# The second layer of a fused attention and MLP kernel, done for two batches at once with two levels of seven products

## The chip, the cores and the metric

The kernel runs on one core of one Trainium2 chip. The metric is the device time of one execution in microseconds (us); the time of a kernel is the median of several runs.

## The reference

Attention with normalised queries and keys is followed by an MLP with two matrix products. There are 8 batches, 12 heads, 448 positions and a head dimension of 64, so the MLP sees 8 x 448 rows of 768 numbers; its inner width is 2048. All is float32 (the weights arrive as float64).

```python
q_n, k_n = (rmsnorm(q, g_q), rmsnorm(k, g_k))
scores = scale * np.matmul(q_n, k_n.transpose(0, 1, 3, 2))
attn = np.exp(scores - np.max(scores, axis=-1, keepdims=True))
attn = attn / (np.sum(attn, axis=-1, keepdims=True) + 1e-09)
x = np.matmul(attn, v)          # then (B,H,S,D) -> (B*S, H*D)
h = x @ w_in                    # 768 -> 2048
g = h - np.tanh(h)
out = g @ w_out                 # 2048 -> 768
```

## The kernel before, in words

**Two streams on one TensorE.** The work is written out by hand in one order, in which each engine keeps its instructions. The attention is cut into 48 steps `s`, one for each batch and pair of heads (six a batch). The MLP of a batch is a Python generator (`hidden`, then `project`; `project_first` for batch 0), which yields after each matmul the time that it should take. The function `slot(s)` (from step 12 on) issues one attention step and calls `run(gap / 2)` eight times in between, which draws MLP matmuls from the generator until their time is used up. `gap_ns` says how much MLP goes into a step: from step 12 on, a sixth of a batch's MLP. The MLP of a batch runs while the attention of the next one is made; the last batch's MLP has no attention beside it.

**A slot.** It opens with the attention block on TensorE: scores of the last keys of step s+1, the values of step s, the division (`divide`, on VectorE, DVE), and the other scores of s+1, whose exponentials ScalarE (ACT) makes. After that comes one piece of DVE work between each two draws of MLP: `add` (L527, L528: sums of the exponentials over the key blocks; two instructions of 128x896), then `norm_blocks` (L458 to L463: mean squares of queries and keys, the power on GpSimd (POOL)), then `add_last` and `fold` (L535, L592, L594, and eight small copies on ACT, L598), `scale_blocks` (L470), two `turn_blocks` (L480, L484) and `spread_sums` (L606 to L611).

**The MLP.** Both layers use a scheme with seven products of half-sized blocks instead of eight (Strassen's, in Winograd's form): rows 0 to 223 and 224 to 447 of the 448 positions are the halves of one operand, halves of the inner dimension and of the output the others. `products` runs them in the `ORDER` 1, 5, 6, 2, 3, 7, 4. In the first layer (`hidden`) a block `j` (of four) has seven products of six matmuls of 224 columns; in the second (`project`) a block `j` (of three) has seven products of eight. Three PSUM banks serve the products in turn: products 1, 5, 6 and 4 take the next bank and start anew, while 2, 3 and 7 go on adding in the banks of 1, 5 and 6 after these have been read. Reading is done by `use` right after a product, on ACT for product 1 and on DVE for most others. For product 2 of the first layer it is `shrink` with `v`, the bank itself (L711 and L712: the tanh on ACT, then a subtraction on DVE, both from PSUM). A part of this work is put in `late["todo"]` and is issued after the next product's matmuls.

**The sums ahead.** The seven products need sums of blocks of the moving operand. For the first layer `divide` makes them when it has both halves (L634 to L637, on POOL). For the second layer `factors` makes them per block `j` (L722, L723 on DVE, L724 and L756 on POOL).

**The weights.** Sums of weights for both layers are made during batch 0 and kept in DRAM. From batch 1 on, tiles of weights come through a ring of six places in SBUF, loaded by SP's queue (`ring_load`, L379); a load is issued when its place has been left, which is four tiles ahead of its use. SP issues all DMAs in the order in which they are written, and waits in that order.

**Results.** `store` (L764) turns a 128x448 tile in 32x32 blocks on DVE and sends it by four DMAs.

Of the kernel before, what the change touches and what calls it, by code (L numbers as in the profile page):

```python
# [20 lines left out]
NCH = 4  # L21
# [116 lines left out]
def bounded_path(tc, ctx, q, k, v, moe_w_in, moe_w_out, out, g_col, ident, ones, half_ones, neg_half, early):  # L138
# [31 lines left out]
    HC, HF = CD // 2, CF // 2  # L170
    SETS = CF // 4
    ORDER = (1, 5, 6, 2, 3, 7, 4)
    SLOTS, SLOT = 6, 8 * P
# [16 lines left out]
    xp = pool("xp", bufs=9)  # L190
    gp = pool("gp", bufs=1)
    wp_stack = ctx.enter_context(ExitStack())
    wp = wp_stack.enter_context(tc.tile_pool(name="wp", bufs=1))
# [9 lines left out]
    def mm_bank():  # L203
        return bank_of("mm")

    loaded = {}

    def load(s, names):
        b, hp = steps[s]
        for name in names:  # L210
            src = {"q": q, "k": k, "v": v}[name]
            if s == 0 and name != "v":
                t = early[name]
            else:
                shape = [CP, 2, NCH, D] if name == "q" else [P, NCH, 2, D] if name == "k" else [P, 2, NCH, D]
                t = nat.tile(shape, F32, name=f"{name}_nat", bufs=3 if name == "v" else 2)
                fetch(nc, name, t, src[b, 2 * hp : 2 * hp + 2], by_blocks(s))
            loaded[name, s] = t
# [7 lines left out]
    }  # L226
    BLOCKS = {1: 0, 2: 1, 4: 2, 7: 3, 5: 4, 6: 5, 3: 6}
    w_out_dram = scratch.tile([P, 7, HC, HF, P], F32, name="w_out")
    w_in_words, w_out_words = weight_words(moe_w_in), weight_words(moe_w_out)
# [135 lines left out]
    def ring_slot():  # L365
# [3 lines left out]

    ring_steps = [  # L370
        (b, layer, j, p)
        for b in range(1, B)
        for layer, count in ((0, SETS), (1, HC))
        for j in range(count)
        for p in ORDER
    ]
    ring_tiles = {}

    def ring_load(to):  # L379

        for n in range(len(ring_tiles), min(to, len(ring_steps))):
            b, layer, j, p = ring_steps[n]
            t = ring_tiles[ring_steps[n]] = ring_slot()
            if layer == 0:
                assert kept[1] > j
                nc.sync.dma_start(out=t[:, : 2 * HALF], in_=w_in_dram[j, p])
            else:
                nc.sync.dma_start(out=t, in_=w_out_dram[:, BLOCKS[p], j].rearrange("p f d -> p (f d)"))

# [49 lines left out]
    def load_blocks(s):  # L439
        b, hp = steps[s]  # L440
        t = loaded["qk", s] = late["blocks"].tile([P, 2, NJ, BL], F32, name="qk_nat", bufs=2)
        for i, src in enumerate((q, k)):
            for h in range(2):
                rows = src[b, 2 * hp + h].rearrange("(j t) (m d) -> m t j d", t=BL, d=BL)
                for m in range(2):
                    r = (2 * h + m) * BL
                    nc.sync.dma_start(out=t[r : r + BL, i], in_=rows[m])
# [20 lines left out]
    def scale_blocks(s):  # L468
        n, rr = normed[s], normed.pop(("rr", s))
        nc.vector.tensor_tensor(  # L470
            out=n.rearrange("p i j d -> p (i j) d"), in0=loaded.pop(("qk", s)).rearrange("p i j d -> p (i j) d"),
            in1=rr[:, :, None].to_broadcast([P, 2 * NJ, BL]), op=ALU.mult,
        )
# [114 lines left out]
    def fold(s):  # L588

        t = sums.pop(s)[0].rearrange("p h s -> p (h s)")  # L590
        turned_sum = late["blocks"].tile([P, 2 * S], F32, name="sum_T")
        nc.vector.transpose(out=turned_sum, in_=t)  # L592
# [20 lines left out]
    def divide(s, av):  # L613
        b, hp = steps[s]
        rs = whole.pop(s)
        x = xT[b, hp] = xp.tile([P, S], F32, name="xT")
        for n in range(2):
# [6 lines left out]
        for c in range(NCH):  # L624
            del probs[s, c]
        if hp < HC:
            return
        c = hp - HC
        if c == 0:
            tt[b] = tp.tile([P, 3, HC, HS], F32, name="tt", bufs=1)  # L630
        eng = nc.vector if b == 0 and c == HC - 1 else nc.gpsimd
        x11, x12, x21, x22 = (xT[b, r][:, n : n + HS] for r in (c, hp) for n in (0, HS))
        t1, t2, t4 = (tt[b][:, i, c] for i in range(3))
        eng.tensor_tensor(out=t1, in0=x12, in1=x11, op=ALU.subtract)  # L634
        eng.tensor_tensor(out=t2, in0=x22, in1=t1, op=ALU.subtract)  # L635
        eng.tensor_tensor(out=x12, in0=x22, in1=x12, op=ALU.subtract)
        eng.tensor_tensor(out=t4, in0=x21, in1=t2, op=ALU.subtract)  # L637

# [15 lines left out]
    def products(b, layer, count, width, depth, moving, done_with):  # L654
# [8 lines left out]
        def product(j, p, bank, first):  # L663
# [20 lines left out]
            for fn in now:  # L684
                fn()

        for j in range(count):
# [8 lines left out]
    def hidden(b):  # L696

        g = late["g"] = gp.tile([P, CF, S], F32, name="gT")
        t2 = late["tg"].tile([P, 3, HF, HS], F32, name="tg") if b else None
        late["t"] = t2  # L700
        x = [xT.pop((b, c)) for c in range(CD)]
        t = tt.pop(b)
        low, high = slice(0, HS), slice(HS, S)
        moving = {
            1: lambda c: x[c][:, low], 2: lambda c: x[c + HC][:, low], 3: lambda c: x[c + HC][:, high],
            4: lambda c: t[:, 2, c], 5: lambda c: t[:, 0, c], 6: lambda c: t[:, 1, c], 7: lambda c: x[c][:, high],
        }

        def shrink(rows, cols, h, eng):
# [4 lines left out]
        def done_with(j):  # L714
# [11 lines left out]
            def use(p, bank):  # L726
                v = view(bank)
                if p == 1:
                    nc.scalar.copy(out=s1, in_=v)
# [14 lines left out]
                elif p == 4:  # L744
                    nc.vector.tensor_tensor(out=s1, in0=v, in1=s1, op=ALU.add)

                    if b and j == SETS - 1:
                        factors()

                    def rest():  # L750
                        shrink(down, low, s1, nc.gpsimd)
                        if b and j < SETS - 1:
                            factors()
                        if b:
                            g21, f2, f4 = g[:, down, low], t2[:, 1, up], t2[:, 2, up]
                            nc.gpsimd.tensor_tensor(out=f4, in0=g21, in1=f2, op=ALU.subtract)  # L756
# [7 lines left out]
    def store(b, n, y):  # L764
# [6 lines left out]
        for i in range(P // BL):  # L771
# [4 lines left out]
            )  # L776

    def project(b):
        g, t = late["g"], late["t"]
# [6 lines left out]
        def done_with(j):  # L786
            y1, y2, s1 = (part(n).rearrange("p f s -> p (f s)") for n in ("s2", "s5", "s1"))

            def use(p, bank):
                v = bank[:, :HS]  # L790
                if p == 1:
                    nc.scalar.copy(out=s1[:, low], in_=v)
# [20 lines left out]
    def project_first(b):  # L813
# [35 lines left out]
        wp_stack.close()  # L849
        late["tg"] = pool("tg", bufs=1)  # L850
        late["blocks"] = pool("blocks", bufs=1)

    def mlp():
        late["todo"], late["keep"] = [], []
        for b in range(B):
            yield from hidden(b)
            yield from project(b) if b else project_first(b)
        for fn in late["todo"]:
            fn()
# [13 lines left out]
    H_NS = 4 * HS / ENGINE_NS * 7 * 6 * SETS  # L873
    O_NS = 4 * HS / ENGINE_NS * 7 * HC * HF

    def gap_ns(s):

        if s < 2 * NP:
            return H_NS / 12 if s % NP < 3 else 4 * S / ENGINE_NS * CD * CF / 12
        return (H_NS + O_NS) / (4 * NP)  # L880

# [477 lines left out]
```

## Time and profile before

| what | value |
|---|---|
| runs | 1421.66, 1422.3, 1425.9 us (median 1422.3) |
| profiled execution, first to last instruction (span) | 1418.0 us |
| PE, busy | 1383.4 us (98%) |
| PE weight load, busy | 1163.8 us (82%) |
| DVE, busy | 919.3 us (65%) |
| POOL, busy | 523.2 us (37%) |
| ACT, busy | 478.8 us (34%) |
| DMA | 249.73 MB, mean 176 GB/s; queue 1 64.2% of 16 engines |
| granted TensorE clock, mean | 0.990 |

The page gives the span of the profiled execution and no separate time for it; the median of the runs is 4.3 us longer than that span. "Busy" is the union of the time that an engine's instructions take; on PE the matmuls overlap, so that its busy time isn't a measure of how near it is to its peak, but a gap in it is a time in which nothing was computed. An f32 matmul appears as two records. The page's slices are 40 equal parts of the span, each digit a busy share in tenths. A line number names the line of the kernel that issued an instruction. In views of waits and in timelines, the arrow in brackets names what ended the idle time before an instruction.

Stages by time: batch 0 with its weights until about 300 us, batch 1 until about 461, then batches 2 to 6 of about 166 us each, and batch 7's MLP alone from 1262 us on.

### The profile page before, as it was taken

Reading aid. Unit: us, or ns where it says so; the run is one execution under the profiler, and the core shown is the slowest. Engines: PE = TensorE matmul, PEld = TensorE weight load, DVE = VectorE, ACT = ScalarE, POOL = GpSimd, SP = SyncE. Lnnn points to the kernel's source line nnn. Section 1 sums busy time; section 2 is a strip of 40 time slices with the busy share of each in tenths; the row PEclk is TensorE's granted clock in tenths of the full one; section 3 lists DMA queues with packets and bytes.
Section 4 is the critical chain, followed back from the end, with each engine's and each line's share of the span. In section 5 each row is a group of like instructions: output and inputs, shape, how many; then the busy total and the mean of one; then the engine's idle time right before and its main releaser. Section 6 shows DMA issues by size and latency. Waiting matters only on the chain.

```text
span 1418.0 us, 25611 instructions
## 1 busy us (share of the span) xinstructions
PE 1383.4 (98%) x9752; PEld 1163.8 (82%) x9752; DVE 919.3 (65%) x1565; ACT 478.8 (34%) x1118; POOL 523.2 (37%) x348
## 2 busy tenths in 40 slices
PE   6999899999999999999999999999999999999997
PEld 3568764478998898898889889988998988899997
DVE  3899788866655687567866668656875678633311
ACT  5765554234322333323332233223332233201100
POOL 4565565223521255214533236212452145401310
PEclk8999999999999999999999999999999999999999
DMA  8669788854566656665657666666566756365663
GB/s 183 156 193 238 244 259 224 236 182 133 173 168 158 171 166 163 173 184 156 176 152 195 157 157 178 178 155 165 163 172 171 178 159 186 113 187 170 191 191 94
DMA packets 355256, 249.73 MB, mean 176 GB/s; under 512 B 266484, under 2 KB 297396, under 8 KB 355124
## 3 DMA queue, kind: packets, MB, share of 16 engines
q1 hardware_dynamic: 355120, 248.00, 64.2%
q8 instruction: 79, 1.29, 0.4%
q14 instruction: 53, 0.43, 0.1%
q10 hardware_dynamic: 4, 0.00, 0.0%
HBM read 214.50 MB, written 33.42 MB: 175 GB/s over the span
## 4 chain that ended last, share of the span: by engine, by line
PE 87%; DVE 5%; DMA 3%; SPq 2%; ACT 2%; issue 1%; POOL 0%; ACTq 0%; DVEq 0%
PE mm L675 64%; PE sc L505 9%; PE sc L557 7%; PE mm L840 4%; PE sc L545 2%; DMA w_f<-w_in 1%; SPq L118 1%; DMA w_raw<-in_moe_w_out_dram 1%; DMA gT<-in_moe_w_in_dram 1%; DVE rs L583 1%; DVE w_out L82 1%; ACT sum_g L598 0%; SPq L265 0%; DMA k_nat<-in_k_dram 0%; POOL w_out L90 0%
## 5 line engine op out<-in xcount | busy, mean ns | idle before, releaser
L675 PE MATMUL mm<-xT,w_f 128*128 128x224 f32 x1392 | 275.6, 354 | 0.0
L675 PEld LDWEIGHTS mm<-xT,w_f 128*128 128x128 f32 x1392 | 262.1, 190 | 9.1 <-issue 7.2
L675 PE MATMUL mm<-gT,w_f 128*128 128x224 f32 x1344 | 263.0, 354 | 0.0
L675 PEld LDWEIGHTS mm<-gT,w_f 128*128 128x128 f32 x1344 | 252.8, 190 | 11.4 <-issue 6.5
L463 POOL TENSOR_TENSOR rr_mine<-rr_mine,neg_half 128x28 f32<-128x28 f32 x30 | 145.1, 4837 | 252.1 <-DVE rr_mine L462 252.1
L675 PE MATMUL mm<-tt,w_f 128*128 128x224 f32 x1044 | 209.4, 354 | 5.4 <-DVE gT L712 5.4
L675 PEld LDWEIGHTS mm<-tt,w_f 128*128 128x128 f32 x1044 | 196.5, 190 | 11.4 <-DVE gT L712 7.5
L675 PE MATMUL mm<-tg,w_f 128*128 128x224 f32 x1008 | 197.7, 352 | 0.0
L712 POOL TENSOR_TENSOR gT<-s,th 128x448 f32<-128x448 f32 x96 | 114.9, 1206 | 214.5 <-ACT th L711 213.6
L675 PEld LDWEIGHTS mm<-tg,w_f 128*128 128x128 f32 x1008 | 190.6, 190 | 0.0
L505 PE MATMUL sc<-qT,kT 64*128 64x448 f32 (+1 forms) x960 | 169.5, 501 | 10.1 <-ACT p_last L510 6.6
L505 PEld LDWEIGHTS sc<-qT,kT 64*128 64x128 f32 (+1 forms) x960 | 71.6, 168 | 82.3 <-issue 61.3
L598 ACT COPY sum_g<-sum 32x14 f32<-32x14 f32 x280 | 56.6, 202 | 224.7 <-DVE sum L594 219.0
L619 DVE TENSOR_TENSOR xT<-sc,rs_T 64x224 f32<-64x224 f32 x140 | 54.4, 389 | 68.6 <-PE sc L557 66.6
L635 POOL TENSOR_TENSOR tt<-xT,tt 128x224 f32<-128x224 f32 x23 | 17.1, 744 | 218.0 <-DVE xT L619 217.9
L510 ACT ACTIVATE p<-sc 128x448 f32<-128x448 f32 x120 | 55.5, 549 | 97.8 <-PE sc L505 97.8
L135 POOL TENSOR_TENSOR rr<-rr,neg_half 112x8 f32<-112x8 f32 (+1 forms) x36 | 59.8, 1682 | 65.2 <-DVE rr L134 65.0
L711 ACT ACTIVATE th<-s 128x448 f32<-128x448 f32 x96 | 55.0, 579 | 84.5 <-DVE s L737 36.1
L557 PE MATMUL sc<-p,v_nat 128*32 128x224 f32 x1344 | 79.9, 355 | 0.0
L840 PE MATMUL mm<-gT,w_out 128*128 128x448 f32 x192 | 74.6, 543 | 0.3 <-POOL w_out L90 0.3
L527 DVE TENSOR_TENSOR rows<-p 128x896 f32<-128x896 f32 x38 | 42.4, 1115 | 42.2 <-ACT p L510 42.2
L840 PEld LDWEIGHTS mm<-gT,w_out 128*128 128x128 f32 x192 | 35.7, 190 | 36.9 <-issue 34.9
(145 smaller groups left out, 1751.2 us busy)
## 6 DMA issues: line engine op xcount, KB each, us to landing
w_f<-w_in SPq DMA_DIRECT2D x196, 384.0 KB, 3.1
w_f<-w_out SPq DMA_DIRECT2D x147, 512.0 KB, 4.0
w_raw<-in_moe_w_out_dram SPq DMA_DIRECT2D x16, 768.0 KB, 5.1
out_dram<-th SPq DMA_DIRECT2D x192, 56.0 KB, 1.9
w_in<-w_out SPq DMA_DIRECT2D x21, 384.0 KB, 6.1
qk_nat<-in_q_dram SPq DMA_DIRECT2D x120, 56.0 KB, 2.4
qk_nat<-in_k_dram SPq DMA_DIRECT2D x120, 56.0 KB, 2.3
gT<-in_moe_w_in_dram SPq DMA_DIRECT2D x32, 192.0 KB, 4.4
```

Source lines behind the costliest of these rows:

```text
L135: nc.gpsimd.tensor_tensor(out=r, in0=r, in1=neg_half[:rows], op=ALU.pow)
L463: nc.gpsimd.tensor_tensor(out=mine, in0=mine, in1=neg_half[:, :1].to_broadcast([P, 2 * NJ]), op=ALU.pow)
L505: nc.tensor.matmul(tiles[h][i * keys : (i + 1) * keys, :n], lhsT=kT[r, c * P : c * P + keys], rhs=qT[r, i * n : (i + 1) * n], start=True, ...
L510: nc.scalar.activation(p[:, h, c if c < 2 else 0, :], tiles[h][:, :n], AF.Exp, scale=1.0 if rr is None else rr[:, 0, 2 * c + h : 2 * c + h ...
L527: nc.vector.tensor_tensor(out=t, in0=p[0], in1=p[1], op=ALU.add)
L557: nc.tensor.matmul(av[n][r : r + BL, :HS], lhsT=v_nat[:, h, c, m * BL : (m + 1) * BL], rhs=p[c][:, h, n * HS : (n + 1) * HS], start=False, ...
L598: nc.scalar.copy(out=acc[h * BL : (h + 1) * BL, g], in_=part[g * BL : (g + 1) * BL, h * NJ : (h + 1) * NJ])
L619: nc.vector.tensor_tensor(out=x[m * D : (m + 1) * D, n * HS : (n + 1) * HS], in0=av[n][m * D : (m + 1) * D, :HS], in1=rs[:, n * HS : (n + ...
L675: nc.tensor.matmul(bank[:, f * HS : (f + 1) * HS], lhsT=w[:, c * width + f, :], rhs=moving[p](c), start=(first and f == 0 and c == 0), sto ...
L711: nc.scalar.activation(th, h, AF.Tanh, bias=0.0, scale=1.0)
L712: eng.tensor_tensor(out=g[:, rows, cols], in0=h, in1=th, op=ALU.subtract)
L840: nc.tensor.matmul(bank[:, :S], lhsT=w_out_row(f, n // HC)[:, n % HC * P : (n % HC + 1) * P], rhs=g[:, f, :], start=(f == 0), stop=(f == C ...
```

## The change

Batches 0 and 1 stay as they were. From the third batch on, the first layer of two batches is done one after the other (`hidden(b)`, `hidden(b + 1)`), into two tiles of `g`, and the second layer then for both at once (`project_pair`). There, the two batches are one half each of the moving operand's positions (448 columns), so the outer seven products work with 448 columns. In each outer product, the output has three chunks of 128: the last is computed directly (eight matmuls of 448 columns), and for the other two the product is split once more into seven inner products of four matmuls of 224 columns. The outer order is 1, 3, 2, 6, 7, 5, 4.

With that come:

- outer sums of `g`, in place, and inner sums into four rotating tiles `u`, on DVE (14 a pair) and POOL (30), placed after products by `outer_plan` and `inner_plan`;
- accumulation of the outer products in two tiles `acc` and `acc2` (`combine_outer`), on DVE;
- sums of weights for the inner products, made once during batch 1 on POOL from weights read back from DRAM, and written to DRAM (`inner_steps`; one step is taken after each product of batches 1 and 2 until it is done);
- ring tiles for the pair: five per outer product;
- `factors` is done only in batch 1; the sums ahead of the first layer (`x_sums`) are made on POOL in the last block of the layer before (for b+1), or in outer product 5 (for b+2);
- `gap_ns`: batch 1's MLP is spread over eight slots instead of six; after that, a cycle of twelve slots has eight for the two first layers (one block `j` each, 42 matmuls) and four for the pair. Batch 1's part is longer by six matmuls, so the cycle runs six matmuls ahead: product 1 of a block stands before the attention block and product 5 after it;
- tiles shared between attention's stages to make room (`qk_rows`, `qk_n` for `fold`).

```diff
+    PAIRED = 2
+    OUTER = (1, 3, 2, 6, 7, 5, 4)
+    HB = HF // 2 * P
+    def ring_order(b, layer, count):
+        return [(b, layer, j, p) for j in range(count) for p in ORDER]
+
+    ring_steps = ring_order(1, 0, SETS) + ring_order(1, 1, HC)
+    for first in range(PAIRED, B, 2):
+        for b in (first, first + 1):
+            ring_steps += ring_order(b, 0, SETS)
+        ring_steps += [(first, 2, p, part) for p in OUTER for part in range(5)]
...
+            elif layer == 2 and p == 0:
+                nc.sync.dma_start(out=t, in_=w_out_dram[:, BLOCKS[j], HC - 1].rearrange("p f d -> p (f d)"))
+            elif layer == 2:
+                n = min(2 * HB, 7 * HB - 2 * (p - 1) * HB)
+                at = 2 * (p - 1) * HB
+                nc.sync.dma_start(out=t[:, :n], in_=inner_dram[j][:, at : at + n])
...
+        turned_sum = late["blocks"].tile([P, 2, NJ, BL], F32, name="qk_n", bufs=1).rearrange("p i j d -> p (i j d)")
...
+        if b < PAIRED and hp >= HC:
+            c = hp - HC
+            x_sums(b, (c,), range(4), nc.vector if b == 0 and c == HC - 1 else nc.gpsimd)
...
+            if b and b <= PAIRED:
+                inner_step()
...
+        ahead = {5: (0,), 6: (1, 2), 4: (3,)} if b >= PAIRED and b % 2 == 0 else {}
...
+                if j == SETS - 1 and p in ahead:
+                    x_sums(b + 1, range(HC), ahead[p], nc.gpsimd)
...
-                        if b and j < SETS - 1:
+                        if single and j < SETS - 1:
                             factors()
...
+    def inner_steps():
...
+            work = (
+                (s1, a21, a22, ALU.add), (s3, a11, a21, ALU.subtract),
+                (s2, s1, a11, ALU.subtract), (s4, a12, s2, ALU.subtract),
+            )
+            for n, (out, x, y, op) in enumerate(work):
+                yield lambda: nc.gpsimd.tensor_tensor(out=out, in0=x, in1=y, op=op)
+                if n == 0 and i + 1 < len(OUTER):
+                    fetch_outer(i + 1)
+            keep(i, 0, a11)
...
+    def project_pair(b):
...
+        outer_plan = {
+            3: {0: [(0, 0, V), (0, 1, V), (1, 0, G)], 5: [(0, 2, V), (1, 1, G)], 2: [(0, 3, V)],
+                3: [(1, 2, V)], 4: [(1, 3, V)]},
+            2: {0: [(2, 0, V), (2, 1, V)], 1: [(2, 2, V)], 5: [(2, 3, V)]},
+            6: {1: [(3, 0, G)], 2: [(3, 1, G)]},
+            7: {1: [(3, 2, G)], 2: [(3, 3, G)]},
+        }
+        inner_plan = {5: 0, 6: 1, 7: 2, 4: 3}
...
+            if q in inner_plan and k + 1 < len(OUTER):
+                inner_sum(OUTER[k + 1], inner_plan[q], G)
+            if p == 5 and b + 2 < B and q in (1, 5, 6, 2):
+                x_sums(b + 2, range(HC), ((1, 5, 6, 2).index(q),), G)
...
+        for k, p in enumerate(OUTER):
+            step = ring_steps.index((b, 2, p, 0))
+            ring_load(step + 5)
+            w = ring_tiles[b, 2, p, 0].rearrange("p (f d) -> p f d", d=P)
+            bank = mm_bank()
+            yield from matmuls(bank, S, lambda i: w[:, i], [rows(p, f, 1, slice(0, S))[:, 0] for f in range(HF)], True)
+            flush()
+            at(k, 0)
+            late["todo"].append(lambda p=p, v=bank[:, :S]: combine_outer(p, HC - 1, v))
...
+            for i, q in enumerate(ORDER):
...
+                yield from matmuls(bank, HS, lambda c: w[:, c], moving, first)
+                flush()
...
+                at(k, q)
...
+        for b in range(PAIRED, B, 2):
+            yield from hidden(b)
+            while late["inner"] is not None:
+                inner_step()
+            yield from hidden(b + 1)
+            yield from project_pair(b)
...
+    AHEAD_NS = 4 * HS / ENGINE_NS * 6
+    PAIR_NS = 4 * HS / ENGINE_NS * 7 * (7 * HF // 2 + 2 * HF)
...
         if s < 2 * NP:
             return H_NS / 12 if s % NP < 3 else 4 * S / ENGINE_NS * CD * CF / 12
-        return (H_NS + O_NS) / (4 * NP)
+        if s < 2 * NP + 8:
+            return (H_NS + O_NS + AHEAD_NS) / 32
+        return (H_NS if (s - 2 * NP - 8) % 12 < 8 else PAIR_NS) / 16
```

## The prediction

> **What bounds the kernel now.** I read the page first, then what TensorE waits for, then the chain in order of time, then the instructions of one stretch.
>
> The page, busy time by engine and the slices of PE and DVE:
>
> ```profile
> PE 1383.4 (98%) x9752; PEld 1163.8 (82%) x9752; DVE 919.3 (65%) x1565; ACT 478.8 (34%) x1118; POOL 523.2 (37%) x348
> PE   6999899999999999999999999999999999999997
> DVE  3899788866655687567866668656875678633311
> ```
>
> TensorE is the bound: from slice 7 on nearly nothing is missing, so matmuls taken out are time taken out, as long as no new wait appears. DVE at 65% is no bound on average.
>
> The chain that ended last, in order of time (start, length, what):
>
> ```profile
> 1210.19 21.39 PE mm L675 x112
> ...
> 1237.65 21.38 PE mm L675 x112
> 1259.58 2.41 PE sc L557 x48
> 1261.99 148.52 PE mm L675 x784
> ```
>
> Two prices come from here. The tail has 784 matmul records in 148.52 us, 189.4 ns each; an f32 matmul of 224 columns has two records, so it costs 378.8 ns, and I call that a unit. And one attention step (a slot) repeats every 1237.65 - 1210.19 = 27.46 us: 56 units (21.2) and an attention block of 6.25 us on TensorE.
>
> What TensorE waits for (total, times, longest), and the stretch in which that happens, batch 6's first slot:
>
> ```profile
> PE mm L675 <- DVE gT L712: 5.4, 6, 1.0
> ```
>
> ```profile
> 1126.78 1.09 DVE L527 TENSOR_TENSOR rows<-p 128x896 f32<-128x896 f32 x1 [1.33 <-ACT p L510]
> ...
> 1127.98 1.09 DVE L528 TENSOR_TENSOR rows<-rows,p_full 128x896 f32<-128x896 f32 x1
> ...
> 1131.35 0.62 DVE L731 TENSOR_TENSOR s<-mm,s 128x448 f32<-128x448 f32 x1 [2.29 <-PE mm L675]
> 1131.89 1.08 DVE L458 TENSOR_REDUCE rr_mine<-qk_n 128x28 f32<-128x896 f32 x1
> 1133.01 0.78 DVE L460 COPY rr_other<-rr_mine 32x28 f32<-32x28 f32 x4
> ...
> 1134.30 4.79 POOL L463 TENSOR_TENSOR rr_mine<-rr_mine,neg_half 128x28 f32<-128x28 f32 x1 [25.08 <-DVE rr_mine L462]
> 1134.66 1.26 DVE L535 TENSOR_TENSOR rows<-rows,p_last 64x448 f32<-64x448 f32 x2
> 1135.96 1.11 DVE L592 STREAM_TRANSPOSE sum_T<-rows 128x896 f32<-128x896 f32 x1
> 1137.11 1.09 DVE L594 TENSOR_REDUCE sum<-sum_T 128x28 f32<-128x896 f32 x1
> 1138.28 1.78 ACT L598 COPY sum_g<-sum 32x14 f32<-32x14 f32 x8 [7.89 <-DVE sum L594]
> 1140.09 0.55 ACT L711 ACTIVATE th<-mm 128x448 f32<-128x448 f32 x1
> 1140.66 0.62 DVE L712 TENSOR_TENSOR gT<-mm,th 128x448 f32<-128x448 f32 x1 [2.47 <-ACT th L711]
> ...
> 1141.34 2.54 PE L675 MATMUL mm<-tt,w_f 128*128 128x224 f32 x12 [1.02 <-DVE gT L712]
> ...
> 1145.62 0.67 DVE L722 TENSOR_TENSOR tg<-gT 128x448 f32<-128x448 f32 x1
> ```
>
> This is the view that decides. Product 4 takes the PSUM bank of product 2, so it waits until the tanh (L711) and subtraction (L712) of product 2 have read it. The tanh stands on ACT behind eight small copies of `fold`, these behind `fold` on DVE (L592, L594), that behind `add_last` (L535) and the norm (L458). A few us of DVE work in the wrong place become a TensorE wait of 1.02 us. It happens once a batch, because a slot is 56 units and a block j of seven products 42, so the two drift against each other and only one slot in six lines up like this.
>
> [...] the tanh's matmul was done at about 1135.6, yet it ran at 1140.09 behind the copies. [...] the L722 above took 0.67 us alone; in an earlier batch, beside GpSimd's L712, it took this:
>
> ```profile
> 672.36 1.55 DVE L722 TENSOR_TENSOR tg<-gT 128x448 f32<-128x448 f32 x1 [1.03 <-POOL gT L712]
> ```
>
> **Removed.** A pair's second layer was 2 x 168 = 336 units. Now each of seven outer products has 8 matmuls of 448 columns (16 units) and 7 x 4 of 224 (28): 7 x 44 = 308. Three pairs save 84 units x 0.3788 = -31.8 us, all on TensorE's path. The 448-column matmul is at L840 32 records in 12.22 us, about 376.6 ns a record after 0.17 of latency, against 2 x 189.4; 336 records x 2.2 ns = -0.7. The five first-slot waits of batches 2 to 6 go with their alignment: -5.1. The sums `factors` made per block from batch 2 on (L722 to L724, L756) go too; DVE and GpSimd get that back, TensorE does not wait for them: 0.
>
> **Moved: hidden slots.** This is the largest term. The slots of the first layer are now exactly 42 units, one block j, so there is no drift: all line up alike. The instruction order of the built program shows how. The attention block stands between product 1 and product 5, and DVE's order is: add of product 5, `add` (two instructions), norm, add of product 6, `add_last`, `fold`, subtraction of product 2. Before, `add` ran while DVE waited for product 5; now it stands behind it. Walk, from the start of product 5: it ends at 6 units = 2.27, DVE starts 0.2 later, at 2.47. From there, start to start in the stretch above: L731 to the next instruction 0.54; the two of `add` 2.35 (1.18 and 1.2 apart, L527 to L528 measured 1.20); L458 to L535 2.77; L535 to L592 1.30; to L594 1.15; to the copies 1.17; to the tanh 1.81; to L712 0.57; to the matmul 0.68. Together 12.34, so product 4 can start at 14.81. TensorE is there after five products, at 5 x 2.273 = 11.37. **Wait 3.44 us in every such slot.** The next product needs the add of product 3, done at about 16.4, and starts at 17.1: no further wait. The divide is reached at about 20.8, before its values (21.9). Full slots of this kind: batches 2, 3, 4, 5 four each, batch 6 two: 18 x 3.44 = +61.9. The third slot of batch 6 has no norm (-2.2): +1.2. The last has no fold: 0. Together +63.1. Bounds: 2.8 us (if `add` is partly covered) to 3.9 a slot, 50 to 71.
>
> **Added: pair slots.** An inner product is 4 units, 1.52 us, so a bank comes back after two products, 3.0 us; in the first layer it was 4.5, in the old second layer 6. DVE per pair: 42 adds of 0.39, 21 of 448 columns (0.61 from PSUM; about 0.75 from SBUF, by L723's mean of 758 ns), 12 transposes of 0.75, 14 sums of 128x896 at 1.2 (L527, L528, L470: 1.12 to 1.37). I walked the four attention slots (77 units each) with these, in the built order. First slot: no wait. Second: ahead of the add of product 5 stand three adds 1.2, four sums 4.8, `add` 2.3, norm 2.3, combine and transpose 1.4, `add_last` 1.3, fold 2.2; DVE is through at 17.1, TensorE wants the bank at 14.3: 2.8, and 0.4 at product 6. Third: 1.5, a combine behind fold. Fourth: DVE's `scale_blocks` waits for the pow (4.8 us) that GpSimd does behind two inner sums (2.4 each, twice L712's 1206 ns) and nine x-sums of 0.75, at about 19; the combine behind it frees its bank at 24.0 instead of 19.3: 4.8. Sum 9.5. [...] half as much again, 14. I take 12 for each of the two pairs with attention: +24, bounds 10 and 40. The last pair has no attention; its products take 16.5 us and GpSimd's share is four to six sums, 10 to 14: +1 for `OUTER` 2's sums. In the three slots in which GpSimd makes x-sums beside `add`: +1.6.
>
> **Added: batch 1.** Seven times 1 MB is read and 1.8 MB written, and GpSimd makes 28 sums of 512 columns, about 1.4 us (1206 x 512/448). SP waits in order for these sums and for the transfers that free their room; behind it stand the ring loads, four tiles (about 9 us of products) ahead, median 3.1 to 4.0 us to landing. GpSimd's shrinks and `factors` stand behind the same sums. DMA share is 0.6 before. Bounds: 0 (all hidden) and 14 (2 us in each of seven rounds). I take +4. Below nothing is excluded: nothing is removed there. Later ring traffic falls (2.3 MB per 44 units against 0.5 per 8): 0, the loads were hidden.
>
> **Tail.** After the last matmul there is one more add of 448 columns: +0.7.
>
> **Sum**, on the profiled execution's span: 1418.0 - 31.8 - 0.7 - 5.1 + 63.1 + 24 + 1 + 1.6 + 4 + 0.7 = 1474.8. The median 1422.3 lies 4.3 above the span: 1479.
>
> **Rivals.** (a) *Faster*: the wait for product 2's bank does not come, because DVE is through `fold` 3.4 us earlier than walked. Against it stands the same chain measured at 1.02 us in five batches; for it, only that the page's averages leave DVE a third of its time. With it gone, the other terms leave 1479 - 63 = 1416; with the pair waits gone as well, 1391. The point from which it decides: gains and losses without it balance at 6 us, so 0.3 us in each of 18 slots. (b) *Half*: the wait is about 2 us: 1479 - 18 x 1.4 = 1454. (c) *Pair stage much worse*: GpSimd's sums and the pow become the bound. By count it has some 24 inner sums, 6 outer, 12 x-sums and 4 pows, 100 us[...] of 150: for it the fourth slot; against it the other slack. 15 us more a pair: 1509. (d) *Batch 1 by DMA*: 14 instead of 4 and as much again on GpSimd: 1500.
>
> **Chances.** Forecast 0.62, (a) 0.11, (b) 0.10, (c) 0.10, (d) 0.07. Adding the bounds as independent gives about 20 either way; the range takes in (b) and most of (c) and (d) and leaves out (a): 1447 to 1508. A measurement of this kernel tells 0.3% (4.3 us) from no change. All cases but (a) end slower; of (a), 0.02 may end within that bound: faster 0.09, same 0.02, slower 0.89.
>
> **What would show it.** Hidden slots of 25.6 us instead of 22.2, with an idle of 3.4 ahead of product 4, released by DVE's subtraction (L751 of the changed kernel), about 19 times. Pair slots of 35 to 41 with idle at products 3 and 6, released by adds. A tail without waits. DVE idle 2.5 us at the start of each hidden slot, waiting for product 5. Wrong, if the hidden slots show no such idle, or if the growth sits in batch 1.

## The result and the profile after

The changed kernel takes 1536.8 us (median of four runs, 1532.9 to 1539.7) against 1422.6 of the kernel before: a ratio of 1.080, with a 95% interval of 1.078 to 1.082. It is slower, as forecast, but by 114 us instead of 57, and outside the range. The profiled execution has a span of 1536.2 us at a mean granted clock of 0.962, against 1418.0 us at 0.990.

Lines of the changed kernel that are named here, with those of the kernel before: `add` L549, L550 (L527, L528), norm L479 to L484 (L458 to L463), `add_last` L557 (L535), `fold` L614, L616 and its copies L620 (L592, L594, L598), scale L492 (L470), tanh and subtraction of product 2 L750, L751 (L711, L712), matmuls of the first layer L706 (L675), matmuls of the pair L925, its adds L932 and GpSimd's sums L892 (outer) and L899 (inner).

The page's busy time, and the slices of PE:

```profile
PE 1405.0 (91%) x9248; PEld 1099.1 (72%) x9248; DVE 1044.8 (68%) x1640; ACT 484.6 (32%) x1130; POOL 718.8 (47%) x418
PE   6999899999999898999889889899989988999997
```

TensorE does 504 records fewer and is nevertheless busy 22 us longer; and the row of nines is broken from slice 14 on. Those are two symptoms: it waits, and what it does takes longer.

What TensorE waits for, in total, times, longest:

```profile
PE mm L706 <- DVE gT L751: 33.1, 12, 3.4
PE mm L925 <- issue: 20.9, 7, 6.7
PE mm L706 <- DVE g L751: 18.9, 6, 3.2
PE mm L706 <- issue: 9.6, 3, 3.3
```

The L706 rows are waits at product 4: 33.1 + 18.9 + 9.6 = 61.6 us in 21 places. Two of them, of 2.03 and 1.11 us, lie in batch 1. The other 19 are the forecast wait, 58.5 us where 63.1 was forecast. The chain of waits in order of time, of one slot (start, length, what) and of the tail:

```profile
1037.75 2.48 PE mm L706 x12
1052.44 6.49 PE mm L706 x24
...
1065.01 2.48 PE mm L706 x12
...
1411.74 116.26 PE mm L925 x504
```

A slot is 1065.01 - 1037.75 = 27.26 us; 25.6 was forecast, and 42 units with an attention block are 22.2 without any wait. The tail's pair takes 116.26 us without a break, for 308 units of 0.3788 (116.7): that much of the change does what it was meant to do. The timeline of that slot:

```profile
1040.32 0.62 DVE L772 TENSOR_TENSOR s<-mm,s 128x448 f32<-128x448 f32 x1 [4.21 <-PE mm L706]
1040.87 1.08 DVE L549 TENSOR_TENSOR rows<-p 128x896 f32<-128x896 f32 x1
...
1049.38 1.78 ACT L620 COPY sum_g<-sum 32x14 f32<-32x14 f32 x8 [9.69 <-DVE sum L616]
...
1051.19 0.54 ACT L750 ACTIVATE th<-mm 128x448 f32<-128x448 f32 x1
1051.76 0.62 DVE L751 TENSOR_TENSOR g<-mm,th 128x448 f32<-128x448 f32 x1 [2.42 <-ACT th L750]
...
1052.44 3.62 PE L706 MATMUL mm<-tt,w_f 128*128 128x224 f32 x12 [3.15 <-DVE g L751]
```

DVE stands idle for 4.21 us in front of the add of product 5 (L772), with `add` (L549) queued behind it. Product 4 starts 14.76 us after product 5 (1037.68), where the walk gave 14.81. But it then takes 3.62 us where twelve records take 2.5 elsewhere. The windows of that stretch give the reason (bounds, length, busy time of PE, PEld, DVE, ACT and POOL, then the granted clock, DMA share and GB/s):

```profile
1052.68:1053.68 1.00, 1.00 (x6) 1.00 (x6) 1.00 (x2) 0.00 (x0) 0.00 (x0) 1.00 0.29 64
1053.68:1054.68 1.00, 1.00 (x4) 0.93 (x4) 1.00 (x3) 0.58 (x1) 0.01 (x1) 0.53 0.18 30
1054.68:1055.68 1.00, 1.00 (x4) 0.88 (x4) 1.00 (x3) 0.00 (x0) 1.00 (x1) 0.50 0.65 106
1055.68:1056.68 1.00, 1.00 (x5) 0.88 (x4) 0.96 (x3) 0.59 (x2) 0.12 (x1) 0.50 0.66 106
```

From 1.3 us after the wait, for 3.4 us (until within the next window, which has 0.76), TensorE is granted half its clock. The wait of 1.02 us in the kernel before, which my walk started from, is followed by full clock (1.00 in each of the five windows from 1140.34 on). So each such slot pays twice: the wait, and 27.26 - 22.2 - 3.15 = 1.9 us of slow matmuls after it.

### The profile page after: what moved, and what is told of

The parts are those of the page before. It is cut to its first block, busy times and chain, and to the rows that moved or that the text cites. A ratio compares the mean times of both kernels' runs of the same rounds, so it can differ in the third digit from the quotient of the medians.

```text
span 1536.2 us, 24843 instructions
## 1 busy us (share of the span) xinstructions
PE 1405.0 (91%) x9248; PEld 1099.1 (72%) x9248; DVE 1044.8 (68%) x1640; ACT 484.6 (32%) x1130; POOL 718.8 (47%) x418
## 4 chain that ended last, share of the span: by engine, by line
PE 63%; DVE 17%; POOL 7%; issue 5%; DMA 3%; ACT 3%; SPq 2%; DVEq 0%; ACTq 0%; POOLq 0%
PE mm L706 24%; PE mm L925 18%; PE sc L527 8%; PE sc L579 5%; PE mm L1075 4%; POOL rr_mine L484 3%; DVE rows L549 2%; ACT sum_g L620 2%; DVE rows L557 2%; DVE rows L550 1%; DVE qk_n L614 1%; DVE rr_mine L479 1%; DVE sum L616 1%; PE sc L567 1%; POOL u L899 1%
## 5 line engine op out<-in xcount | busy, mean ns | idle before, releaser
L706 PE MATMUL mm<-tt,w_f 128*128 128x224 f32 x1044 | 235.6, 384 | 61.6 <-DVE gT L751 33.1
L484 POOL TENSOR_TENSOR rr_mine<-rr_mine,neg_half 128x28 f32<-128x28 f32 x30 | 147.1, 4903 | 293.8 <-DVE rr_mine L483 292.6
L706 PEld LDWEIGHTS mm<-tt,w_f 128*128 128x128 f32 x1044 | 209.3, 204 | 85.2 <-DVE gT L751 37.3
L706 PE MATMUL mm<-xT,w_f 128*128 128x224 f32 x1104 | 226.0, 360 | 0.0
L706 PEld LDWEIGHTS mm<-xT,w_f 128*128 128x128 f32 x1104 | 216.0, 197 | 6.2 <-issue 3.9
L527 PE MATMUL sc<-qT,kT 64*128 64x448 f32 (+1 forms) x960 | 172.3, 500 | 15.7 <-ACT p_last L532 8.8
L925 PE MATMUL mm<-u,w_f 128*128 128x224 f32 x672 | 143.2, 365 | 29.9 <-issue 20.9
L620 ACT COPY sum_g<-sum 32x14 f32<-32x14 f32 x280 | 56.3, 201 | 318.8 <-DVE sum L616 312.9
L925 PEld LDWEIGHTS mm<-u,w_f 128*128 128x128 f32 x672 | 130.8, 197 | 35.7 <-issue 26.1
L925 PE MATMUL mm<-gT,w_f 128*128 128x224 f32 (+1 forms) x480 | 135.0, 434 | 4.5 <-DVE s L932 4.5
L527 PEld LDWEIGHTS sc<-qT,kT 64*128 64x128 f32 (+1 forms) x960 | 71.0, 167 | 92.1 <-issue 60.6
L925 PEld LDWEIGHTS mm<-gT,w_f 128*128 128x128 f32 x480 | 92.4, 194 | 44.3 <-issue 37.2
L751 POOL TENSOR_TENSOR gT<-s,th 128x448 f32<-128x448 f32 x60 | 73.7, 1236 | 100.3 <-ACT th L750 95.8
L925 PE MATMUL mm<-g,w_f 128*128 128x224 f32 (+1 forms) x360 | 100.6, 436 | 0.0
L751 POOL TENSOR_TENSOR g<-s,th 128x448 f32<-128x448 f32 x36 | 42.6, 1189 | 115.8 <-ACT th L750 111.3
L772 DVE TENSOR_TENSOR s<-mm,s 128x448 f32<-128x448 f32 x32 | 20.0, 624 | 106.6 <-PE mm L706 106.6
L925 PEld LDWEIGHTS mm<-g,w_f 128*128 128x128 f32 x360 | 70.0, 196 | 29.1 <-issue 28.3
L750 ACT ACTIVATE th<-s 128x448 f32<-128x448 f32 x96 | 53.9, 572 | 91.1 <-DVE s L782 63.5
```

What stands on the lines that cost most here:

```text
L484: nc.gpsimd.tensor_tensor(out=mine, in0=mine, in1=neg_half[:, :1].to_broadcast([P, 2 * NJ]), op=ALU.pow)
L527: nc.tensor.matmul(tiles[h][i * keys : (i + 1) * keys, :n], lhsT=kT[r, c * P : c * P + keys], rhs=qT[r, i * n : (i + 1) * n], start=True, ...
L620: nc.scalar.copy(out=acc[h * BL : (h + 1) * BL, g], in_=part[g * BL : (g + 1) * BL, h * NJ : (h + 1) * NJ])
L706: nc.tensor.matmul(bank[:, f * HS : (f + 1) * HS], lhsT=w[:, c * width + f, :], rhs=moving[p](c), start=(first and f == 0 and c == 0), sto ...
L750: nc.scalar.activation(th, h, AF.Tanh, bias=0.0, scale=1.0)
L751: eng.tensor_tensor(out=g[:, rows, cols], in0=h, in1=th, op=ALU.subtract)
```

## The experiments

All of them start from the changed kernel. Times are medians; ratios are against the kernel before, on the same chip. Runs 1 to 4, 5 to 7, 8 to 10 and 11 had a chip each; the kernel before took 1420.6 to 1421.8 us on them. My theory after the result: the order on DVE's and ACT's queues makes the wait (as forecast), the wait makes the clock drop (not forecast), and in the pair DVE's instructions take longer beside GpSimd's long sums. The rivals: the forecast wait is a by-product of some other bound, so that removing it moves little; the slow matmuls come from their weights or the memory traffic, not from the wait; the excess lies in batch 1.

**1. `add` first.** In `slot`, the sums of exponentials (and ACT's squares, `square_blocks`) come ahead of the first eighth of the matmuls, so DVE does the sums while it would wait for product 5:

```diff
         blocks = by_blocks(s + 2)
-        run(gap / 2)
         if has(s + 1):
             add(s + 1)
         if blocks:
             square_blocks(s + 2)
         run(gap / 2)
+        run(gap / 2)
```

> The changed kernel with one move: in each slot, the two sums of add and the squares are issued ahead of the first draw of matmuls, so that DVE has them before product 5's add instead of behind it. Queue-order theory: the chain from product 5 to product 4 loses the two instructions (2.35 us), product 4 can start at 12.5 instead of 14.8 us, the wait falls from 3.2 to about 1.1 us, and after so short a gap the TensorE clock stays full: a first-layer slot of 23.3 us instead of 27.26, 18 times 3.9 = -70, about 1467 us. Rival (DVE has simply too much to do in these slots, whatever its order): the work comes late elsewhere, slots of 26 to 27 us, 1515 to 1537 us.

Measured: 1457.5 us, ratio 1.025 (1.021 to 1.029), 79 us less. A first-layer slot is 23.4 us. The wait ahead of product 4:

```profile
526.98 2.54 PE L706 MATMUL mm<-tt,w_f 128*128 128x224 f32 x12 [0.93 <-DVE gT L751]
```

0.93 us of wait, and 2.54 us for the twelve records, as behind the wait of 1.02 us in the kernel before: the clock stays. The place of two instructions in DVE's order (ACT's squares moved with them) was worth 79 us: 18 slots by 3.9 are 70, the two pairs with attention give 11, and batch 2 begins 3 us later. That a wait shorter by 2.2 us makes a slot shorter by 3.9 is the second half of the theory, which the next run takes alone.

**2. Fill the wait.** The wait stays, but TensorE is kept busy in it by matmuls whose result nobody reads:

```diff
...
+            if layer == 0 and p == 4 and PAIRED <= b < B - 1:
+                spare = banks_of_sc()
+                for _ in range(8):
+                    nc.tensor.matmul(spare[:, :HS], lhsT=w[:, 0], rhs=moving[p](0), start=True, stop=True)
```

> The changed kernel with eight more matmuls of 224 columns ahead of product 4 in the first layers of batches 2 to 6, into a free bank that nobody reads (3.0 us of work more in each block). Clock theory: the wait for product 2's bank stays, but TensorE isn't idle in it, the granted clock stays at 1.0 behind it (0.5 for about 3.4 us in the changed kernel), and a slot takes 25.5 instead of 27.26 us: 18 times 1.75 = -31, about 1506 us, though there is more work. Rival (the matmuls behind the gap are slow for want of weights [...]): slots of 27 us or more, 1537 to 1545 us.

Measured: 1517.3 us, ratio 1.067 (1.062 to 1.072); slots of 25.6 us instead of 27.26. The timeline:

```profile
500.65 3.19 PE L710 MATMUL sc<-tt,w_f 128*128 128x224 f32 x16
504.02 2.54 PE L713 MATMUL mm<-tt,w_f 128*128 128x224 f32 x12 [0.18 <-DVE gT L758]
```

Three us of useless work more in each slot, and the slot is 1.7 us shorter: product 4 can't start earlier, but it runs at full clock (1.00 in each of the three windows of 1 us from 503.02 on). Its weights, its inputs and the work of the other engines are as they were, so the drop of these slots hangs on TensorE's idle time. In sum it gives 20 us where 31 was expected: batch 6's first layer, where the fill also stands in two slots with a short wait or none, comes out 1.7 us longer, and the two pairs, which the edit leaves alone, 6 us longer.

**3. Without GpSimd's inner sums.** The inner products that need one take a block of `g` as it is.

> The changed kernel without GpSimd's 24 inner sums per pair; the inner products that need them use a block of g as it is. [...] DVE's instructions with two SBUF inputs in the pair slots go back to what they take alone (128x896 about 1.1 us, 128x448 about 0.65), and the norm's power is no longer behind the sums; a pair stage with attention falls from 165 to about 150 us (142 without any wait), -30 in all, about 1507 us. Rival (DVE's number of instructions alone makes the waits): at most -5 a pair, 1527 us or more.

```diff
...
+            if eng is not V:
+                us[p, i] = x11
+                return
```

Measured: 1499.0 us, ratio 1.054 (1.051 to 1.057), 38 us less. A pair with the slot before it is 177.8 us against 193.9. DVE's adds with both inputs in SBUF (L932) fall from 1.62 to 0.66 us in the mean. The gain is larger than expected: most of the pair's excess hangs on these sums. It isn't that they keep the power waiting: in the eight pair slots of the changed kernel the power starts at most 0.54 us after its input, and DVE stands idle in front of the scaling that needs it (L492) for at most 0.10 us. Run 6 changes only the length of GpSimd's instructions.

**4. Without the sums of weights in batch 1.** Nothing is read back, summed or written; the pair loads blocks of the outer weights of the same size instead.

> The changed kernel without the making of the inner weights in batch 1 (no reading back, no sums on GpSimd, no writing); the pair loads blocks of the outer weights of the same size in their place. If the sums, SP's waits or the transfers are what slows batch 1, its stage falls by about 10 us: 1527 us. If it is only the slots' new spacing: no change, 1537 us.

```diff
...
-        late["inner"] = inner_steps()
+        late["inner"] = None
```

Measured: 1530.8 us, ratio 1.077 (1.073 to 1.080), 6 us less. The sums cost more than the 4 forecast, but they aren't where the 57 us went: that rival falls.

**5. The small copies later.** Added to run 1: the eight copies of `fold` on ACT, behind which the tanh of product 2 stood, come one piece later (`gather_sums`, after the next `run(gap / 2)`).

```diff
...
         run(gap / 2)
+        if folded:
+            gather_sums(s + 1)
         if blocks:
             scale_blocks(s + 2)
```

> The kernel with add ahead (the run before this one), and fold's eight small copies on ACT issued one piece later, behind product 2's tanh. Queue-order theory: the tanh no longer stands behind them, the bank is free about 10.2 us after product 5's start, before TensorE wants it at 11.4, and a first-layer slot takes 22.3 instead of 23.4 us: 18 times 1.1 = -20, about 1437 us. Rival (the wait's last link is DVE's fold or the power, not the copies): no change, 1457 us.

Measured: 1429.2 us, ratio 1.0068 (1.0043 to 1.0094), 28 us less, 23 of them in the first layers. The tanh now precedes the copies, product 4 starts without a wait, and a slot is 22.17 us, which is what 42 units and the attention block need:

```profile
516.94 0.55 ACT L755 ACTIVATE th<-mm 128x448 f32<-128x448 f32 x1 [5.16 <-PE mm L711]
...
519.27 1.78 ACT L625 COPY sum_g<-sum 32x14 f32<-32x14 f32 x8 [1.78 <-DVE sum L616]
...
521.22 2.43 PE L711 MATMUL mm<-tt,w_f 128*128 128x224 f32 x12
```

**6. GpSimd's sums in pieces.** Added to run 5: GpSimd's sums of 128x896 in the pair become four of 128x224. The work stays the same, only the length of one instruction changes.

```diff
-            eng.tensor_tensor(out=out, in0=a, in1=z, op=ALU.subtract)
+            cuts = [(c, h) for c in range(2) for h in (low, high)] if eng is nc.gpsimd else [(slice(0, 2), slice(0, S))]
+            for c, h in cuts:
+                eng.tensor_tensor(out=out[:, c, h], in0=a[:, c, h], in1=z[:, c, h], op=ALU.subtract)
...
-            eng.tensor_tensor(out=u, in0=a, in1=z, op=ALU.subtract)
+            for c in range(KB) if eng is nc.gpsimd else ():
+                eng.tensor_tensor(out=u[:, c], in0=a[:, c], in1=z[:, c], op=ALU.subtract)
+            if eng is nc.vector:
+                eng.tensor_tensor(out=u, in0=a, in1=z, op=ALU.subtract)
```

> The kernel of the run before, and GpSimd's inner and outer sums of the pairs each in four pieces of 128x224 instead of one of 128x896. [...] DVE waits at most one piece, 0.6 instead of 2.1 us; its 128x896 sums in the pair slots come down from up to 3.0 to at most 1.7 us, and each pair stage with attention loses 5 to 10 of its some 20 us of waits: about 1422 us (1415 to 1430). Rival ([...] GpSimd becomes the bound with four times as many instructions): same or slower, 1437 us or more.

Measured: 1420.8 us, ratio 1.0001 (0.9992 to 1.0010), 8 us less, 7 of them in the two pairs with attention. The groups of instructions show what the length of GpSimd's instructions does to DVE. DVE's adds with both inputs in SBUF, in the changed kernel and in run 5 (count, busy us, mean ns, idle before):

```profile
L932 DVE TENSOR_TENSOR acc<-acc,s 128x448 f32<-128x448 f32 x18 | 29.2, 1624 | 0.6
```

```profile
L937 DVE TENSOR_TENSOR acc<-acc,s 128x448 f32<-128x448 f32 x18 | 25.2, 1399 | 0.8
```

and in run 6, with the same GpSimd work in pieces:

```profile
L942 DVE TENSOR_TENSOR acc<-acc,s 128x448 f32<-128x448 f32 x18 | 14.3, 792 | 0.8
```

From run 5 to run 6 the mean falls from 1.40 to 0.79 us, beside 0.61 for the same add with one input from PSUM. Not every instruction gains: the norm's four copies (L481) took 0.78, 1.87 and 2.57 us in the last three slots of run 5's first pair, and take 2.00, 2.13 and 2.17 here. GpSimd itself pays too: its busy time grows from 709 us in run 5 to 766. The 8 us are less than run 3's 38, which also took 167 us of work off GpSimd (718.8 to 551.6 busy) and started from a kernel with all its long waits.

**7. The directly computed chunk first.** Added to run 6:

```diff
             flush()
+            combine_outer(p, HC - 1, bank[:, :S])
             at(k, 0)
-            late["todo"].append(lambda p=p, v=bank[:, :S]: combine_outer(p, HC - 1, v))
```

> The kernel of the run before, and in each outer product the combination of the chunk that was computed directly is issued right behind its matmuls, ahead of the outer sums and of the first inner product. Theory (inner product 6 waits for this bank, which DVE reads late): 1 to 3 us less in the second to fourth slot of each pair with attention, 1412 to 1420 us. Rival (DVE then idles in front of the matmuls and all behind it comes later): 1425 us or more.

Measured: 1424.9 us, ratio 1.0035 (1.0020 to 1.0049), slower than run 6. The expected gain isn't there; the wait in the second slot of the pair grows from 2.39 to 4.44 us, that in the fourth from 4.45 to 5.38, and the eight records behind them take 3.36 us (1.78 in run 6) and 3.33 us (3.32). The order in the changed kernel is the better one here.

**8 to 10. Other orders in the pair, and batch 1 in halves.** Run 8 moves DVE's outer sums for outer product 2 and spreads the sums of x; run 9 also issues the last product's direct chunk first; run 10 also halves GpSimd's instructions in batch 1:

```diff
-            2: {0: [(2, 0, V), (2, 1, V)], 1: [(2, 2, V)], 5: [(2, 3, V)]},
+            2: {0: [(2, 0, V), (2, 1, V)], 5: [(2, 2, V)], 6: [(2, 3, V)]},
...
-            if p == 5 and b + 2 < B and q in (1, 5, 6, 2):
-                x_sums(b + 2, range(HC), ((1, 5, 6, 2).index(q),), G)
+            if q == 4 and b + 2 < B and p in (2, 6, 7, 5):
+                x_sums(b + 2, range(HC), ((2, 6, 7, 5).index(p),), G)
...
+            if p == 4:
+                combine_outer(p, HC - 1, bank[:, :S])
             flush()
             at(k, 0)
-            late["todo"].append(lambda p=p, v=bank[:, :S]: combine_outer(p, HC - 1, v))
+            if p != 4:
+                late["todo"].append(lambda p=p, v=bank[:, :S]: combine_outer(p, HC - 1, v))
...
-                yield lambda: nc.gpsimd.tensor_tensor(out=out, in0=x, in1=y, op=op)
+                yield lambda: [
+                    nc.gpsimd.tensor_tensor(out=out[:, h], in0=x[:, h], in1=y[:, h], op=op)
+                    for h in (slice(0, HB // 2), slice(HB // 2, HB))
+                ]
```

> The run with copies late and GpSimd's sums in pieces, with two more moves inside the pair: VectorE's third and fourth sum for outer product 2 (chunks (2,2) and (2,3)) come one and two inner products later, so that none of them stands ahead of the add of inner product 5; and the four groups of GpSimd's sums of x for the batch after next, which all lay inside outer product 5, lie one each behind inner product 4 of outer products 2, 6, 7 and 5. If the waits left in the pair are those of the two in-order queues (4.5 us in two places behind VectorE, 10.9 us in four behind GpSimd, in the trace of the run before this one), most of these 15 us go: about 1408 to 1413. [...] the same sums only collide elsewhere: 1419 to 1422, no gain.

> The run of the later sums, and for the last outer product alone the combination of its directly computed chunk is issued before the combination that is still owed from the product before, not behind it. If the wait in the last slot of the pair is that of VectorE's queue, it shortens by one add of 448 columns, 1 to 2 us, twice: 2 to 4 us under the run of the later sums. If the order of two adds on a queue that is not the last to end matters nothing: within 1 us of it. If the bank's release isn't what is late, but the buffer into which the result is added, it waits there as it did when all combinations came first: 1 to 3 us over.

> The run above, and GpSimd's 28 sums of the inner weights in batch 1 in two instructions each of half the length. [...] 2 to 5 us less than the run above, at most the 6 us that leaving those sums out gave. If GpSimd's added start costs outweigh it: 0 to 2 us more.

Measured: 1419.3 us, ratio 0.9991 (0.9981 to 1.0001); 1418.1 us, ratio 0.9981 (0.9972 to 0.9990); 1412.5 us, ratio 0.9947 (0.9928 to 0.9965). Run 8 misses its forecast. In its trace the waits that I had moved are gone, but others have grown: the first pair's waits sum to 9.6 us in run 6 (1.52, 2.39, 0.24, 1.00, 4.45), to 9.6 in run 8 (1.52, 1.38, 1.86, 1.57, 1.00, 2.26) and to 9.4 in run 9; what changes is the granted clock, in the mean of the profiled execution 0.987, 0.989 and 0.992. Run 10 gives back about 5 us of batch 1: the first product after the attention of step 20 starts at 479.7 us instead of 484.9 in run 9, nearly all that run 4 gave by leaving the sums out. It is the best version, 0.5% (0.35 to 0.72%) faster than the kernel before, which is a small gain but clear of the noise.

**11. `add` back behind the matmuls, in the pair's slots alone.** Added to run 10, since DVE stands idle 2.0 us ahead of `add` in these slots:

```diff
+        first_piece = s >= 2 * NP + 8 and (s - 2 * NP - 8) % 12 >= 8
+        if first_piece:
+            run(gap / 2)
         if has(s + 1):
             add(s + 1)
         if blocks:
             square_blocks(s + 2)
-        run(gap / 2)
+        if not first_piece:
+            run(gap / 2)
         run(gap / 2)
```

> The best run so far (halved sums of the inner weights), and in the four attention slots of each pair alone the two instructions of the sums of the exponentials (and the squares) go back to where the changed kernel had them, behind the first eighth of the slot's matmuls. In the runs before, the waits of a pair add to 9.6 us whichever sums are moved, and VectorE stands idle 2.0 us in each pair slot in front of those sums, waiting for ScalarE's exponentials, with the adds of the pair queued behind. If that idle time is what the pair's waits are made of: up to 2 us in each of eight slots, 4 to 12 us under the run before, 1400 to 1408. If the waits come from the order further on in the slot (the norm, the fold, and what stands behind GpSimd's power), or if the adds then stand in front and the sums collide with GpSimd's pieces instead: within 3 us of it, either way.

Measured: 1418.5 us, ratio 0.9980 (0.9967 to 0.9994): some 5 us slower than run 10, which neither reading had expected. Two of the waits of run 10's first pair:

```profile
711.88 1.78 PE L938 MATMUL mm<-gT,w_f 128*128 128x224 f32 x8 [1.38 <-DVE s L945]
...
752.35 1.75 PE L938 MATMUL mm<-u,w_f 128*128 128x224 f32 x8 [1.58 <-POOL rr_mine L484]
```

and two of this run's:

```profile
711.67 3.33 PE L938 MATMUL mm<-u,w_f 128*128 128x224 f32 x8 [4.34 <-issue]
756.99 3.08 PE L938 MATMUL mm<-u,w_f 128*128 128x224 f32 x8 [3.31 <-POOL rr_mine L484]
```

The sum of the waits hardly changes (10.2 us in three places against 9.5 in six), but the three long waits are each followed by slow matmuls, eight records in 2.3 to 3.3 us instead of 1.75, while of the six short ones only the last, of 2.11 us, is (3.08 us). Run 11's batch 1 also ends 1.7 us later, for no reason that lies in its edit, so not all of the 5 us is this.

## Why the prediction was right in direction and wrong in size

**Removed: right.** The last pair's 308 units took 116.26 us in the tail, 116.7 by the price used; the first-slot waits of their old kind are gone.

**Moved, hidden slots: the wait right, its price too low.** The step "Wait 3.44 us in every such slot" holds: 3.1 to 3.4 us in each of the 18, 58.5 in the 19 places against 63.1. What failed is that the wait was taken as the whole price of the slot: a slot lost 5.05 us, not 3.44. The same group of matmuls, product inputs from `tt`, in the changed kernel and in run 6, which has no waits there from batch 2 on:

```profile
L706 PE MATMUL mm<-tt,w_f 128*128 128x224 f32 x1044 | 235.6, 384 | 61.6 <-DVE gT L751 33.1
```

```profile
L711 PE MATMUL mm<-tt,w_f 128*128 128x224 f32 x1044 | 209.9, 355 | 1.9 <-DVE gT L756 1.9
```

25.7 us more for the same 1044 records; the group with inputs from `xT` grows by 6.4 (226.0 against 219.6). These 32 us are the clock: one stretch of 3.41 us at half clock behind each of the 18 waits comes to 30.7. The stretches of the first layers say the same: 219.9 and 219.4 us for eight slots each (177.6 unstalled), and 74.9 for the three of batch 6 (63.4 in run 5, which has no such waits), 95.6 over in all, against 63.1 forecast. In the trace of before, the wait of this kind was 1.02 us, with a clock of 1.00 behind it; behind all 18 waits of 3.1 to 3.4 us it was 0.50, and in the pair behind one of 2.09 us as well (0.50 in each of the three windows of 1 us from 1149.40 on).

**Added, pair slots: the term mis-sized.** Forecast 24, and 1.6 for the sums of x; measured 165.2 and 166.2 us for four slots of 35.4 each, so 48. The first slot, walked without a wait, has one of 2.02 us. Those of the second were walked fairly well (0.4 and 2.8; measured 1.56 and 2.38), the third and fourth came out longer (1.5 and 4.8; measured 3.97 and 6.74). The timeline of the third slot of the changed kernel:

```profile
791.61 2.96 POOL L899 TENSOR_TENSOR u<-g 128x896 f32<-128x896 f32 x1 [6.26 <-PE mm L925]
792.56 2.50 DVE L932 TENSOR_TENSOR acc<-acc,s 128x448 f32<-128x448 f32 x1
...
795.09 2.38 DVE L932 TENSOR_TENSOR acc<-acc,acc 128x448 f32<-128x448 f32 x1
```

A sum of 448 columns that I took at 0.75 takes 2.4 to 2.5 us, because it runs beside an inner sum and ends only after it: the first inner sum ends at 794.57 and the first add 0.49 us later, the second at 796.99 and the second add 0.48 later. In the fourth slot the step "DVE's `scale_blocks` waits for the pow" failed: the power ends at 848.40, and DVE, busy until then and after, reaches the scaling (L492) at 850.12. It is late because what stands ahead of it takes longer beside GpSimd's sums (`add`'s first sum 2.35 us instead of 1.09, the norm's copies 3.25 instead of 0.78), and the add behind it takes 2.49. I took "half as much again" for what runs beside GpSimd's sums; for such adds it was a factor of 2.2 in the mean (1.62 us) and 3.3 at worst. That the price went with the length of GpSimd's instructions, not with a fixed share, is what the ends above and runs 3 and 6 show: 0.66 us without the inner sums, and 0.79 instead of 1.40 with the same work in pieces. And behind the waits of 3.97 and 6.74 us the matmuls are slow here too: eight records take 3.33 and 3.24 us, at a granted clock of 0.50. Which order would make the last 9.6 us of waits in a pair go stays open: six versions (runs 6 to 11) left it between 9.4 and 10.2 us, and I have not found what holds it.

**Added, batch 1: too low.** Forecast 4 of 0 to 14. Leaving the sums out gave 6, halving the instructions about 5; which points to the length of GpSimd's instructions, more than to SP's queue, which was the reason I gave.

**The sum.** -37.6 removed, +95.6 hidden slots, +48 pairs, +6 batch 1 and +0.7 after the last matmul are +112.7; the span grew by 118.2. Of the 5.5 us left over, 4.2 lie ahead of batch 1, whose first product starts at 296.9 us instead of 292.7; in the traces of all runs that start lies between 292.7 and 298.6.

**The rivals.** (a), at 1416 without the first-layer wait, was the right price for another kernel: run 5 has no such wait and takes 1429, with the pairs' mis-sized term in the difference. (b) fell: the wait was 3.15 us, not 2. (c) was half right: the pairs cost 22 us more than forecast, but GpSimd isn't their bound. It stands idle for over 90 us in all in front of its inner sums (L899), and splitting the sums raises its total and still gains; the cost is what single sums do to DVE (its adds, 1.62 us in the mean against 0.66 without them). (d) was small.

## What to carry to other kernels

When a change makes all repetitions of a stage alike, walk one of them through every engine's order of instructions; a wait that was rare may then come every time, and moving two instructions can remove it. Look at the granted clock behind a wait of TensorE before pricing it at its length: here a wait of 3.15 us cost a slot 5.05, and of two pairs with nearly the same sum of waits, one had slow matmuls behind each of three long ones (10.2 us), the other behind one of six short ones (9.5 us). Where GpSimd and DVE work in SBUF at the same time, price DVE's instructions by what they take beside GpSimd's, not alone, and try cutting GpSimd's into pieces before moving it: here that brought DVE's adds from 1.40 to 0.79 us.

## What the runs showed of the hardware that had not been expected

- The length of a wait alone did not tell whether the clock drops. Behind each of the 18 first-layer waits of 3.1 to 3.4 us in the changed kernel lies a stretch of 3.41 us at 0.50; behind 0.93 us in run 1 the twelve records took 2.54 us, as at full clock. In the pair, waits of one length went either way: behind 2.38 us the next eight records took 1.78 us in the changed kernel and 2.58 in run 1, and behind 2.09 us 1.78 in run 6 and 2.91 in run 1. What decides between them was not shown.
- Useless matmuls made the kernel faster: eight in each wait, 3.0 us of work, shortened a slot by 1.7 us.
- DVE's copies took longer beside GpSimd's sums as well: four copies of 32x28 (L481) took at most 0.78 us in every pair slot of run 3, and up to 3.25 us beside GpSimd's sums in the changed kernel.
